# Converting 64-bit float weights inside an attention and MLP-mixer kernel: sign kept in the mantissa word, exponent masked in place, and the steps spread over four turns

## The chip, the cores and the metric

The kernel runs on one core of one Trainium2 chip. The metric is the device time of one execution in microseconds (us), as the median of several runs. Five engines of the core work side by side, each through its own list of instructions in order: TensorE (PE in the profile; PEld is its weight load), VectorE (DVE), ScalarE (ACT), GpSimd (POOL) and SyncE (SP). In this kernel SP issues nearly all the DMAs. An engine that meets an instruction whose input isn't ready stands still with everything behind it in its list.

## The reference

```python
def _attn_ref(q, k, v, g_q, g_k):                 # batch 8, heads 12, seq 448, head_dim 64
    q_n, k_n = rmsnorm(q, g_q), rmsnorm(k, g_k)
    scores = 1.0 / np.sqrt(64) * q_n @ k_n.transpose(0, 1, 3, 2)
    attn = softmax(scores)
    return attn @ v
def _moe_ref(x, w_tok1, w_tok2, w_ch1, w_ch2):    # x: the heads side by side, 8 x 448 x 768
    h = np.maximum(x.transpose(0, 2, 1) @ w_tok1, 0.0) @ w_tok2
    u = x + h.transpose(0, 2, 1)
    return u + np.maximum(u @ w_ch1, 0.0) @ w_ch2
```

(Shortened; the softmax has its maximum subtracted.) q, k and v are float32. The four weights are float64: `w_tok1` 448 x 256, `w_tok2` 256 x 448, `w_ch1` 768 x 1536 and `w_ch2` 1536 x 768. The kernel sees their bits as 64-bit integers, and has to make float32 of them itself.

## The kernel before

All 48 pairs of heads (six for each batch element) go through attention; each batch element then goes through the token layers (`tok1`, `tok2`) and the two channel layers. For batch element 0 the channel layers are plain products (`first_stage`, 36 of them); for the seven others they are a scheme with seven products of sums of blocks (`ch1`, `ch2`), for which sums of weight blocks must lie in DRAM. Attention for batch element b+1 runs in between the mixer work of element b. TensorE, VectorE, ScalarE and GpSimd get their instructions in the order in which the code emits them. Lists of work items are woven into each other by `merge`, by the costs written beside the items. SP's own queue is ordered by the scheduler of the framework.

**The weight conversion.** The weights come in 40 chunks of at most 128 rows and 512 numbers: chunks 0 to 3 are `w_tok1` and `w_tok2`, chunks 4 to 39 feed the 36 plain products of batch element 0 ("stage n" is chunk n+4). A chunk lies in one of five `raw` buffers as pairs of 32-bit words, so that the low words and the high words each lie 8 bytes apart. Per chunk there are six computing steps:

1. VectorE, line 263, *mask*: mantissa bits of the high word, with the implied one, into `cv_sb` (two buffers).
2. VectorE, line 264, *sum*: low word times 2^-32 plus that mantissa, into the low word.
3. VectorE, line 266, *exponent*: exponent bits of the high word into the same `cv_sb` buffer, which lies packed.
4. ScalarE, line 274, *shift of the exponent*: a Relu with scale 8 and a bias, in place in `cv_sb`.
5. VectorE, line 281, *sign*: sign bit of the high word joined to the result of step 4, into the high word.
6. VectorE, line 308, *product*: low word times 2^-20 times high word, into the float32 stage.

`weight_items` makes "turns" of these. Turn i issues, in this order: the load of chunk i+2 (line 176, on SP, two DMAs; the buffer is that of chunk i-3), sign of chunk i-2, mask, sum and exponent of chunk i, shift of chunk i-1, product of chunk i-2, and the store of the stage of chunk i-3 to DRAM (line 192, on SP).

Turns 0 to 13 are woven into the first attention steps. In `first_items`, five turns (14 to 18) are woven into the token layers of batch element 0; the others are hung on the 36 products: turn 19+k behind product number `begins(k)`, from k = 0 to 23. Stage k+13 is so made at place k, well ahead of its product at first and a few products ahead at the end. The last six products are woven with the last sums of weight blocks (`sum_items`): GpSimd forms them (lines 204 to 207), SP sends them out (line 211) and fetches earlier stages back (line 240).

Other lines that the steps below touch: 391 the exponentials on ScalarE, 361 and 739 transposes on TensorE, 387, 440 and 460 its attention products, 761 and 769 its token products, 774 the addition of a token product on VectorE, 857 the plain products on TensorE, 866 and 867 the copy (ScalarE) and the addition (GpSimd) of their results, 1314 and 1322 to 1325 the start of an inverse root on VectorE and its three Newton steps on GpSimd, 349 the scaling that uses it, 428 the sums of exponentials, 978 the transposes of a finished output on VectorE, 722 the fetch of x for the token layers.

Of the kernel before, what the change touches and what calls it, by code (L numbers as in the profile page):

```python
# [8 lines left out]
F32 = mybir.dt.float32  # L9
U32 = mybir.dt.uint32  # L10
I32 = mybir.dt.int32
I64 = mybir.dt.int64
AF = mybir.ActivationFunctionType
ALU = mybir.AluOpType
# [12 lines left out]
def merge(*lists):  # L27

    totals = [sum(c for c, _ in l) or 1.0 for l in lists]
    done = [0.0] * len(lists)  # L30
    at = [0] * len(lists)
    res = []
    while True:
        live = [i for i in range(len(lists)) if at[i] < len(lists[i])]
        if not live:
            return res
        i = min(live, key=lambda i: (done[i] + lists[i][at[i]][0] / 2) / totals[i])
        c, fn = lists[i][at[i]]
        at[i] += 1
        done[i] += c  # L40
        res.append((c, fn))
# [3 lines left out]
def whole(ctx, tc, shifted, pre, q, k, v, g_q, g_k, moe_w_tok1, moe_w_tok2, moe_w_ch1, moe_w_ch2, out):  # L45


    nc = tc.nc
# [51 lines left out]
    ident, one_c, expo_c, g_t = pre.ident, pre.one_c, pre.expo_c, pre.g_t  # L100
# [3 lines left out]
    cv_sb = const.tile([P, 2, WCOLS], F32, name="cv_sb")  # L104
# [5 lines left out]
    st = dict(pre.st)  # L110
# [43 lines left out]
    def columns(i):  # L154
        src = chunks[i][1][0]
        return WCOLS if chunks[i][2] is None or len(src.shape) == 3 else src.shape[-1]
# [4 lines left out]
    def weight_load(i):  # L161
        rows, srcs, dst = chunks[i]
        wide = srcs[0].dtype == I64
        t = raw_tile()
        flat = t[0:rows].rearrange("p n w -> p (n w)")
        if not wide:
            t = t[:].rearrange("p n w -> p (n w)").bitcast(F32)
            flat = t[0:rows]
        n = columns(i) // len(srcs) * (1 + wide)
        for k, src in enumerate(srcs):  # L170
            to = flat[:, k * n:(k + 1) * n]
            if wide:
                src = src.bitcast(U32)
            if len(src.shape) == 3:
                to = to.rearrange("p (i n) -> p i n", i=src.shape[1])
            nc.sync.dma_start(out=to, in_=src)
        st["raw", i] = t

    def slots(j, lo, hi):

        w, group, m, t = stages[j]
        if group < 3:
            a = ws1[group, lo:hi, :, t, m % 2, :]
        elif group == 3:
            a = ws3[lo:hi, :, t, :]
        else:
            a = ws2[t // 3, lo:hi, :, t % 3, m, :]
        return a.rearrange("q p n -> p q n")

    def store(j):  # L190

        nc.sync.dma_start(out=slots(j, 0, 4), in_=st["stage", j])
# [4 lines left out]
    def sum_items():  # L197
# [39 lines left out]
        def one(i):  # L237
            if i < len(order):
                t = st["sum", order[i]] = raw_tile()
                nc.sync.dma_start(out=eight(t)[:, 0:4], in_=slots(order[i], 0, 4))  # L240
            if 0 <= i - 2 < len(order):
                q = eight(st["sum", order[i - 2]])
                make(q, q)
            if 0 <= i - 3 < len(order):
                send(order[i - 3])
                load_units(st["at"])

        def eight(t):
            if len(t.shape) == 4:
# [3 lines left out]
                [(1.0, lambda i=i: direct(i)) for i in range(n - 6, n + 1)],  # L253
                [(1.0, lambda i=i: one(i)) for i in range(len(order) + 3)])

    def convert_first(i):

        if chunks[i][1][0].dtype != I64:
            return
        rows, n = chunks[i][0], columns(i)  # L260
        lo, hi = (st["raw", i][0:rows, 0:n, w] for w in range(2))
        e = cv_sb[0:rows, i % 2, 0:n].bitcast(U32)
        nc.vector.tensor_scalar(e, hi, 0x000FFFFF, 0x00100000, ALU.bitwise_and, ALU.bitwise_or)  # L263
        nc.vector.scalar_tensor_tensor(  # L264
            out=lo.bitcast(F32), in0=lo, scalar=2.0**-32, in1=e, op0=ALU.mult, op1=ALU.add)
        nc.vector.tensor_scalar(e, hi, 0x7FF00000, None, ALU.bitwise_and)
        st["cv", i] = e

    def convert_second(i):

        if chunks[i][1][0].dtype != I64:
            return
        rows, n, e = chunks[i][0], columns(i), st["cv", i]
        nc.scalar.activation(out=e, in_=e, func=AF.Relu, bias=expo_c[0:rows, 0:1], scale=8.0)

    def convert_bits(i):

        if not 0 <= i < len(chunks) or chunks[i][1][0].dtype != I64:
            return
        hi, e = st["raw", i][0:chunks[i][0], 0:columns(i), 1], st.pop(("cv", i))  # L280
        nc.vector.scalar_tensor_tensor(  # L281
            out=hi, in0=hi, scalar=0x80000000, in1=e, op0=ALU.bitwise_and, op1=ALU.bitwise_or)

    def stage_home(j):


        if j == 8:
            st["stages"] = tu_pool.tile([P, 4, KC, HS], F32, name="stages", tag="tu")
        if 8 <= j < 13:
            o = (j - 8) * 4 * P  # L290
            return st["stages"][:].rearrange("p a b n -> p (a b n)")[:, o:o + 4 * P]
        if 13 <= j < 15:
            return h1_pool.tile([P, C], F32, name="stage", tag="h1")[:, 0:4 * P]
        t = unit_pool.tile([P, 3, 2, P], F32, name="stage", tag="unit")
        return t[:].rearrange("p t i n -> p (t i n)")[:, 0:4 * P]

    def convert_last(i):
        rows, srcs, dst = chunks[i]
        n = columns(i)
        if dst is None:  # L300
            dst = stage_home(i - len(first))
            st["stage", i - len(first)] = dst.rearrange("p (q n) -> p q n", q=4)
        t = st.pop(("raw", i))
        if srcs[0].dtype != I64:
            nc.gpsimd.tensor_copy(out=dst, in_=t[0:rows, 0:n])
        else:
            lo, hi = (t[0:rows, 0:n, w].bitcast(F32) for w in range(2))
            nc.vector.scalar_tensor_tensor(  # L308
                out=dst, in0=lo, scalar=2.0**-20, in1=hi, op0=ALU.mult, op1=ALU.mult)

    def weight_items(lo, hi):

        def one(i):
            if 3 <= i and i + 2 < len(chunks):
                weight_load(i + 2)
            convert_bits(i - 2)
            if i < len(chunks):
                convert_first(i)
            if 0 <= i - 1 < len(chunks):
                convert_second(i - 1)  # L320
            if 0 <= i - 2 < len(chunks):
                convert_last(i - 2)
            if 0 <= i - 3 - len(first):
                store(i - 3 - len(first))
        return [(1.0, lambda i=i: one(i)) for i in range(lo, hi)]


# [652 lines left out]
    def turns(b, cs, send=True):  # L980

        def one(cc):
            trans_y(b, cc)
            if send:
                later(2.0, lambda: send_y(b, cc, st.pop(("y", cc))))
        return [(0.3, lambda cc=cc: one(cc)) for cc in cs]

    def y_order(b):

        return [o * KC + m for m in ((0, 1, 2) if b else (2, 0, 1)) for o in range(2)]  # L990
# [31 lines left out]
    def first_items(tok, prods, some):  # L1022


        convert = weight_items(BEFORE, len(chunks) + 3)
        items = merge(tok, convert[:5])
        for j, it in enumerate(prods[:-6]):
            items.append(it)
            items += [(0.0, convert[5 + k][1]) for k in range(len(convert) - 5) if begins(k) == j]
            if j % 2 and j < 2 * len(some):  # L1030
                items.append(some[j // 2])
            if j in (26, 28):

                items += turns(0, [y_order(0)[j // 2 - 13]])
        return items, prods[-6:]

    def begins(k):


        return 2 + -(-k * 14 // 10) if k < 10 else min(k + 9, 29)  # L1040
# [14 lines left out]
    first, second = weight_chunks()  # L1055
    chunks = first + second
    AHEAD = 1
    BEFORE = len(first) + 10
# [12 lines left out]
    for p in (4, 5):  # L1071
# [7 lines left out]
        out=g_t[:, 0:1], in0=g_t[:, 0:1], scalar=float(D) ** 0.5, in1=g_t[:, 1:2],  # L1079
        op0=ALU.mult, op1=ALU.mult)  # L1080
# [26 lines left out]
    for b in range(B):  # L1107
# [20 lines left out]
        lo = (b + AHEAD) * per + 1  # L1128
# [12 lines left out]
        elif b + AHEAD < B:  # L1141
            t = (b + AHEAD) * NPAIR // 2
# [201 lines left out]
def kernel(  # L1344
# [30 lines left out]
    with tc.If(nc.values_load(small[0:1, 0:1], min_val=0, max_val=1,  # L1375
                              skip_runtime_bounds_check_because="a comparison's result") > 0) as arm:
        whole(tc, False, pre, *args)
    with arm.Else():
        whole(tc, True, pre, *args)
# [30 lines left out]
```

## Time and profile before

| | |
|---|---|
| median of 3 runs | 1311.29 us (1311.14 to 1311.92) |
| the profiled execution's own time | 1311.52 us |
| its span, first to last instruction | 1309.7 us |
| TensorE busy | 1263.6 us (96%) |
| VectorE busy | 764.4 us (58%) |
| ScalarE busy | 372.1 us (28%) |
| GpSimd busy | 352.8 us (27%) |
| first and last mask of the conversion | 24.7 and 257.0 us |

Some 1.8 us of the profiled time lie outside its span. The conversion lives in the first 263 us; the remaining 1047 us are seven rounds of mixer and attention that do not touch it. A row of a timeline is: start (us from the span's start), duration (us), engine, line, operation, output and inputs, shapes, count; in brackets the idle time of the engine before it and what ended it. [...]

### The profile page before, as it was taken

What the parts mean: (1) busy time and instruction counts of PE and PEld (TensorE: products, weight loads), DVE (VectorE), ACT (ScalarE), POOL (GpSimd) and SP (SyncE); (2) the same over time, 40 slices, a digit from 0 to 9 for tenths busy, and PEclk for the clock granted to TensorE, in tenths of its full rate; (3) what the DMA queues carried; (4) which work ended last, traced back from release to release, by engine and by line L of the source; (5) the groups of instructions that cost most, each with busy time, mean ns of one, the idle gap of its engine ahead of it and who ended that gap; (6) DMA issues with size and microseconds to landing.
All of it is one profiled execution on the core that took longest, in us unless ns stands there. A gap on an engine that the chain in (4) does not pass through costs nothing.

```text
span 1309.7 us, 20218 instructions
## 1 busy us (share of the span) xinstructions
PE 1263.6 (96%) x7408; PEld 930.4 (71%) x7408; DVE 764.4 (58%) x1205; ACT 372.1 (28%) x740; POOL 352.8 (27%) x575
## 2 busy tenths in 40 slices
PE   5999999799998999999999999999999999999997
PEld 3344444347687688796778777896788868797996
DVE  6888688937684466645665366654756266433212
ACT  5562433213331134302441044302332033200100
POOL 1203230357342122221332122321232123111220
PEclk9999999899999999999999999999999999999998
DMA  9664487999989676695648667684767865386554
GB/s 212 170 185 134 135 212 177 202 258 252 245 195 233 149 184 160 147 232 118 160 128 222 152 147 178 162 226 101 169 156 166 212 139 141 116 217 135 174 172 91
DMA packets 502449, 228.06 MB, mean 174 GB/s; under 512 B 374532, under 2 KB 464004, under 8 KB 502340
## 3 DMA queue, kind: packets, MB, share of 16 engines
q1 hardware_dynamic: 489218, 224.83, 69.7%
q10 hardware_dynamic: 12994, 1.84, 0.8%
q8 instruction: 61, 1.00, 0.3%
q14 instruction: 48, 0.39, 0.1%
q0 software_dynamic: 128, 0.00, 0.0%
HBM read 187.07 MB, written 39.52 MB: 173 GB/s over the span
## 4 chain that ended last, share of the span: by engine, by line
PE 79%; DVE 8%; DMA 5%; SPq 3%; issue 2%; ACT 1%; POOL 1%; DVEq 0%; ACTq 0%; POOLq 0%
PE m_ps L885 25%; PE m_ps L942 24%; PE o_ps L460 8%; PE s_ps L387 8%; PE m_ps L769 5%; PE m_ps L761 5%; DVE raw L264 1%; PE m_ps L857 1%; PE d_ps L440 1%; DVE raw L281 1%; DMA raw<-in_moe_w_ch_dram 1%; DMA qk_t<-in_k_dram 1%; PE m_ps L440 1%; DVE cv_sb L263 1%; DVE stage L308 1%
## 5 line engine op out<-in xcount | busy, mean ns | idle before, releaser
L942 PE MATMUL m_ps<-hb,unit 128*128 128x224 f32 x1764 | 339.8, 353 | 3.6 <-DMA unit<-ws 1.9
L942 PEld LDWEIGHTS m_ps<-hb,unit 128*128 128x128 f32 x1764 | 332.2, 190 | 14.7 <-issue 12.7
L885 PE MATMUL m_ps<-tu,unit 128*128 128x224 f32 x1008 | 202.0, 355 | 0.1
L885 PEld LDWEIGHTS m_ps<-tu,unit 128*128 128x128 f32 x1008 | 188.9, 190 | 14.8 <-issue 9.2
L391 ACT ACTIVATE e<-s_ps 128x448 f32<-128x448 f32 x294 | 138.1, 549 | 199.7 <-PE s_ps L387 191.5
L885 PE MATMUL m_ps<-uT,unit 128*128 128x224 f32 x756 | 151.2, 354 | 1.0 <-DVE hb L890 1.0
L885 PEld LDWEIGHTS m_ps<-uT,unit 128*128 128x128 f32 x756 | 142.2, 190 | 8.1 <-issue 4.6
L387 PE MATMUL s_ps<-qkT 64*64 64x448 f32 x1260 | 142.0, 545 | 0.0
L460 PE MATMUL o_ps<-e,v 64*64 64x448 f32 x1148 | 131.1, 538 | 0.1
L428 DVE TENSOR_TENSOR es<-es,e 128x896 f32<-128x896 f32 x90 | 109.0, 1212 | 16.6 <-ACT e L391 11.9
L951 POOL TENSOR_TENSOR uT<-uT,r 128x448 f32<-128x448 f32 (+1 forms) x56 | 56.6, 1020 | 228.8 <-DVE r L951 142.7
L890 DVE TENSOR_TENSOR r<-m_ps,r 128x448 f32<-128x448 f32 x63 | 39.2, 622 | 108.3 <-PE m_ps L885 56.2
L951 DVE TENSOR_TENSOR uT<-uT,m_ps 128x448 f32<-128x448 f32 (+1 forms) x70 | 33.7, 499 | 111.2 <-PE m_ps L942 111.2
L387 PEld LDWEIGHTS s_ps<-qkT 64*64 64x64 f32 x1260 | 44.8, 132 | 66.5 <-issue 58.5
L460 PEld LDWEIGHTS o_ps<-e,v 64*64 64x64 f32 x1148 | 45.8, 133 | 63.9 <-issue 59.0
L890 POOL TENSOR_TENSOR hb<-r,r 128x448 f32<-128x448 f32 x21 | 24.6, 1173 | 234.1 <-ACT r L906 234.1
L761 PE MATMUL m_ps<-x,w_sb 112*128 112x384 f32 x256 | 84.5, 487 | 1.0 <-ACT x L741 1.0
L769 PE MATMUL m_ps<-w_sb,h 128*128 128x448 f32 x192 | 75.2, 544 | 3.3 <-DVE uT L774 3.3
L761 PEld LDWEIGHTS m_ps<-x,w_sb 112*128 112x128 f32 x256 | 48.4, 190 | 34.3 <-ACT x L741 1.3
L891 ACT ACTIVATE hb<-hb 128x448 f32<-128x448 f32 x63 | 36.3, 577 | 116.4 <-DVE hb L890 97.2
L1292 DVE TENSOR_REDUCE ms<-sq 128x28 f32<-128x896 f32 (+2 forms) x44 | 47.5, 1079 | 34.1 <-ACT sq L1278 31.3
L857 PE MATMUL m_ps<-hb,stage 128*128 128x448 f32 x144 | 57.2, 556 | 8.0 <-ACT r L866 8.0
(122 smaller groups left out, 1352.7 us busy)
## 6 DMA issues: line engine op xcount, KB each, us to landing
unit<-ws SPq DMA_DIRECT2D x294, 384.0 KB, 4.1
raw<-in_moe_w_ch_dram SPq DMA_DIRECT2D x72, 256.0 KB, 3.6
v<-in_v_dram SPq DMA_DIRECT2D x96, 112.0 KB, 3.7
xs<-xt SPq DMA_DIRECT2D x56, 168.0 KB, 4.6
x<-xs SPq DMA_DIRECT2D x14, 672.0 KB, 7.3
out_dram<-turned SPq DMA_DIRECT2D x168, 56.0 KB, 2.0
qk_t<-in_q_dram SPq DMA_DIRECT2D x144, 56.0 KB, 3.5
qk_t<-in_k_dram SPq DMA_DIRECT2D x144, 56.0 KB, 3.8
```

Of the source, the lines that this page charges most:

```text
L387: nc.tensor.matmul(out=pss[i][rows_of(i, a), 0:S], lhsT=qkT[h, 1, k * D:(k + 1) * D], rhs=qkT[h, 0, :], start=True, stop=True)
L391: nc.scalar.activation(out=e[:, i, :], in_=pss[i][:, 0:S], func=AF.Exp)
L428: nc.vector.tensor_tensor(out=es[:], in0=(es if k > 1 else st["e", t, 0])[:], in1=st["e", t, k][:], op=ALU.add)
L460: nc.tensor.matmul(out=st["o", p][a * D:(a + 1) * D, 0:S], lhsT=vt[rows, k * D:(k + 1) * D], rhs=e[rows, :], **kw)
L761: nc.tensor.matmul(out=ps[:, 0:HC], lhsT=w1_sb[0:R, c, jc * P:(jc + 1) * P], rhs=st["x", b, h][0:R, :, c, :], start=(c == 0), stop=(c == N ...
L769: nc.tensor.matmul(out=ps[:, 0:S], lhsT=st["h1", jc][:, cc * P:(cc + 1) * P], rhs=w2_sb[:, jc].rearrange("p c r -> p (c r)"), start=(jc == ...
L857: nc.tensor.matmul(out=ps, lhsT=a[:, o + 2 * half, :], rhs=natural(half)[:, :, t, :] if wide else u[:, half * KC + t, :], start=(t == 0 an ...
L885: nc.tensor.matmul(out=ps[:, j * HS:(j + 1) * HS], lhsT=w[:, t, j, :], rhs=m, start=(t == 0), stop=(t == KC - 1))
L890: add = lambda e, o, x, y: e.tensor_tensor(out=o, in0=x, in1=y, op=ALU.add)
L942: nc.tensor.matmul(out=ps[:, j * HS:(j + 1) * HS], lhsT=st["w"](j, t), rhs=hb[:, HB[what], t, :], start=(t == 0), stop=(t == KF - 1))
L951: add = lambda e, o, x, y: e.tensor_tensor(out=o, in0=x, in1=y, op=ALU.add)
L1292: self.nc.vector.tensor_reduce(out=st["ms", p][:, p % 2, lo:hi], in_=sq[:, lo:hi], axis=AX_X, op=ALU.add)
```

## The change

The sign goes into the low word right after the sum, and the exponent is masked in place in the high word; the `cv_sb` buffer then serves only between mask and sum. The shift on ScalarE works in place in the high word, two turns behind the mask (it was one). The product stands at the head of the turn, three turns behind the mask (it was two, at the turn's end), ahead of the load into the buffer that it frees. The store follows one turn later, so that there is one turn more; six turns (14 to 19) are woven into the token layers instead of five, and turn 20+k stands at place k.

```diff
     def convert_first(i):
-        rows, n = chunks[i][0], columns(i)
-        lo, hi = (st["raw", i][0:rows, 0:n, w] for w in range(2))
-        e = cv_sb[0:rows, i % 2, 0:n].bitcast(U32)
-        nc.vector.tensor_scalar(e, hi, 0x000FFFFF, 0x00100000, ALU.bitwise_and, ALU.bitwise_or)
-        nc.vector.scalar_tensor_tensor(
-            out=lo.bitcast(F32), in0=lo, scalar=2.0**-32, in1=e, op0=ALU.mult, op1=ALU.add)
-        nc.vector.tensor_scalar(e, hi, 0x7FF00000, None, ALU.bitwise_and)
-        st["cv", i] = e
+        if wide(i):
+            lo, hi = words(i)
+            m = cv_sb[0:chunks[i][0], i % 2, 0:columns(i)].bitcast(U32)
+            nc.vector.tensor_scalar(m, hi, 0x000FFFFF, 0x00100000, ALU.bitwise_and, ALU.bitwise_or)
+            nc.vector.scalar_tensor_tensor(
+                out=lo.bitcast(F32), in0=lo, scalar=2.0**-32, in1=m, op0=ALU.mult, op1=ALU.add)
+            nc.vector.scalar_tensor_tensor(
+                out=lo, in0=hi, scalar=0x80000000, in1=lo, op0=ALU.bitwise_and, op1=ALU.bitwise_or)
+            nc.vector.tensor_scalar(hi, hi, 0x7FF00000, None, ALU.bitwise_and)
 
     def convert_second(i):
-        nc.scalar.activation(out=e, in_=e, func=AF.Relu, bias=expo_c[0:rows, 0:1], scale=8.0)
-
-    def convert_bits(i):
-        nc.vector.scalar_tensor_tensor(
-            out=hi, in0=hi, scalar=0x80000000, in1=e, op0=ALU.bitwise_and, op1=ALU.bitwise_or)
+        if wide(i):
+            e = words(i)[1]
+            nc.scalar.activation(out=e, in_=e, func=AF.Relu, bias=expo_c[0:chunks[i][0], 0:1], scale=8.0)
...
     def weight_items(lo, hi):
         def one(i):
+            if 0 <= i - 3 < len(chunks):
+                convert_last(i - 3)
             if 3 <= i and i + 2 < len(chunks):
                 weight_load(i + 2)
-            convert_bits(i - 2)
-            if i < len(chunks):
-                convert_first(i)
-            if 0 <= i - 1 < len(chunks):
-                convert_second(i - 1)
-            if 0 <= i - 2 < len(chunks):
-                convert_last(i - 2)
-            if 0 <= i - 3 - len(first):
-                store(i - 3 - len(first))
+            convert_first(i)
+            convert_second(i - 2)
+            if 0 <= i - 4 - len(first):
+                store(i - 4 - len(first))
...
-        convert = weight_items(BEFORE, len(chunks) + 3)
-        items = merge(tok, convert[:5])
+        convert = weight_items(BEFORE, len(chunks) + 4)
+        items = merge(tok, convert[:6])
         for j, it in enumerate(prods[:-6]):
             items.append(it)
-            items += [(0.0, convert[5 + k][1]) for k in range(len(convert) - 5) if begins(k) == j]
+            items += [(0.0, convert[6 + k][1]) for k in range(len(convert) - 6) if begins(k) == j]
```

`words(i)` gives the low and the high words of chunk i, `wide(i)` says whether chunk i exists and is 64-bit.

More of the change, by code (lines that the diff above doesn't have):

```diff
@@ L254, in sum_items, with wide, words @@
                 [(1.0, lambda i=i: one(i)) for i in range(len(order) + 3)])
+    def wide(i):
+        return 0 <= i < len(chunks) and chunks[i][1][0].dtype == I64
+    def words(i):
+        return [st["raw", i][0:chunks[i][0], 0:columns(i), w] for w in range(2)]
     def convert_first(i):
-        if chunks[i][1][0].dtype != I64:
-            return
-        rows, n = chunks[i][0], columns(i)
-        lo, hi = (st["raw", i][0:rows, 0:n, w] for w in range(2))
-        e = cv_sb[0:rows, i % 2, 0:n].bitcast(U32)
-        nc.vector.tensor_scalar(e, hi, 0x000FFFFF, 0x00100000, ALU.bitwise_and, ALU.bitwise_or)
-        nc.vector.scalar_tensor_tensor(
-            out=lo.bitcast(F32), in0=lo, scalar=2.0**-32, in1=e, op0=ALU.mult, op1=ALU.add)
-        nc.vector.tensor_scalar(e, hi, 0x7FF00000, None, ALU.bitwise_and)
-        st["cv", i] = e
-    def convert_second(i):
[L271 to L274, printed above, removed]
-    def convert_bits(i):
[L278 to L281, printed above, removed]
-            out=hi, in0=hi, scalar=0x80000000, in1=e, op0=ALU.bitwise_and, op1=ALU.bitwise_or)
+        if wide(i):
[7 more added lines that the diff above has]
+            nc.vector.tensor_scalar(hi, hi, 0x7FF00000, None, ALU.bitwise_and)
+    def convert_second(i):
+        if wide(i):
+            e = words(i)[1]
+            nc.scalar.activation(out=e, in_=e, func=AF.Relu, bias=expo_c[0:chunks[i][0], 0:1], scale=8.0)
     def stage_home(j):
@@ L302, in convert_last @@
             st["stage", i - len(first)] = dst.rearrange("p (q n) -> p q n", q=4)
[L303 to L307, printed above, removed]
+        if wide(i):
+            lo, hi = (w.bitcast(F32) for w in words(i))
             nc.vector.scalar_tensor_tensor(
                 out=dst, in0=lo, scalar=2.0**-20, in1=hi, op0=ALU.mult, op1=ALU.mult)
+        else:
+            nc.gpsimd.tensor_copy(out=dst, in_=st["raw", i][0:rows, 0:n])
+        st.pop(("raw", i))
     def weight_items(lo, hi):
         def one(i):
+            if 0 <= i - 3 < len(chunks):
+                convert_last(i - 3)
             if 3 <= i and i + 2 < len(chunks):
                 weight_load(i + 2)
-            convert_bits(i - 2)
-            if i < len(chunks):
-                convert_first(i)
-            if 0 <= i - 1 < len(chunks):
-                convert_second(i - 1)
-            if 0 <= i - 2 < len(chunks):
-                convert_last(i - 2)
-            if 0 <= i - 3 - len(first):
-                store(i - 3 - len(first))
+            convert_first(i)
+            convert_second(i - 2)
+            if 0 <= i - 4 - len(first):
+                store(i - 4 - len(first))
         return [(1.0, lambda i=i: one(i)) for i in range(lo, hi)]
```

## The prediction

> **What bounds the kernel now.** I read the page first, then busy time by stretch, then TensorE's own timeline for the places where it stands still. Columns of the stretches: length, then PE, PEld, DVE, ACT and POOL busy (instructions), PE clock, DMA share, GB/s.
>
> ```profile
> 20.00:85.00 65.00, 59.67 (x563) 28.58 (x558) 54.61 (x94) 39.79 (x80) 10.20 (x32) 1.00 0.73 191
> 85.00:123.30 38.30, 36.15 (x205) 17.60 (x204) 34.09 (x50) 17.60 (x35) 9.82 (x20) 1.00 0.46 131
> 123.30:199.00 75.70, 75.63 (x340) 34.83 (x336) 54.37 (x80) 27.91 (x52) 19.88 (x36) 1.00 0.69 183
> 199.00:263.00 64.00, 55.96 (x192) 26.38 (x189) 58.49 (x99) 16.84 (x32) 14.06 (x16) 0.95 0.80 188
> ```
>
> TensorE is full from 123 to 199 us and nearly full elsewhere; VectorE comes close in 85 to 123 (89%) and 199 to 263 (91%). So time can be won only where TensorE idles, and VectorE must not be pushed where it is full. TensorE's idle places that have to do with the conversion:
>
> ```profile
> 53.35 1.90 PE L361 MATMUL t_ps<-ident,hb 112*128 112x112 f32 x16 [2.31 <-ACT e L391]
> ...
> 231.74 12.29 PE L857 MATMUL m_ps<-hb,stage 128*128 128x448 f32 x32
> 250.66 20.05 PE L857 MATMUL m_ps<-hb,stage 128*128 128x448 f32 x48 [6.63 <-ACT r L866]
> ```
>
> Both idles are ended by ScalarE. Its timeline says why ScalarE was late:
>
> ```profile
> 52.15 0.72 ACT L274 ACTIVATE cv_sb<-cv_sb,expo_c 128x512 uint32<-128x512 uint32 x1 [2.56 <-DVE cv_sb L266]
> ...
> 249.47 0.72 ACT L274 ACTIVATE cv_sb<-cv_sb,expo_c 128x512 uint32<-128x512 uint32 x1 [8.22 <-DVE cv_sb L266]
> 250.10 0.94 ACT L866 COPY r<-m_ps 128x448 f32<-128x448 f32 x2
> ```
>
> ScalarE stands 8.22 us before a shift whose exponent VectorE has not made; the copies that free TensorE's result buffers are queued behind. In all, the table of waits from 20 to 270 us has this pair at 41.7 us in 14 waits. Most of it costs nothing; at TensorE I count 1.1 us at 27 (same cause, ScalarE waits 3.19), 2.3 at 51, 0.6 at 73, and the 6.63 at 244. The last has a sequel:
>
> ```profile
> 231.74:234.84 3.10, 3.10 (x8) 1.62 (x9) 1.00 1.08 256
> 250.66:253.76 3.10, 3.10 (x4) 1.51 (x5) 0.50 0.92 158
> ```
>
> Behind the gap the clock is 0.50, and 4 matmuls of line 857 begin in 3.10 us instead of 8: about 1.6 us more.
>
> **VectorE's work per turn.** One turn where nothing else intervenes:
>
> ```profile
> 230.24 0.70 DVE L281 SCALAR_TENSOR_TENSOR raw<-raw,cv_sb 128x512 uint32<-128x512 uint32 x1
> 230.98 0.43 DVE L263 TENSOR_SCALAR cv_sb<-raw 128x512 uint32<-128x512 uint32 x1
> 231.45 0.69 DVE L264 SCALAR_TENSOR_TENSOR raw<-raw,cv_sb 128x512 f32<-128x512 uint32 x1
> 232.18 0.43 DVE L266 TENSOR_SCALAR cv_sb<-raw 128x512 uint32<-128x512 uint32 x1
> 232.52 0.68 DVE L308 SCALAR_TENSOR_TENSOR stage<-raw 128x512 f32<-128x512 f32 x1
> 233.12 0.69 DVE L281 SCALAR_TENSOR_TENSOR raw<-raw,cv_sb 128x512 uint32<-128x512 uint32 x1
> ```
>
> From start to start: sign 0.74, mask 0.47, sum 0.73, exponent 0.34, product 0.60: 2.88 us. An instruction that needs the one just before it starts 0.04 us after its end; one that doesn't starts some 0.09 before. The new order is product 0.60, mask 0.47, sum 0.73, sign 0.74 (it reads the sum), exponent 0.34 if the next instruction is free of it: again 2.88. Five operations are removed and five added per chunk; the sum is zero.
>
> Unknown is the exponent mask written in place, 8 bytes apart. No row has it. Nearest is line 263, which reads words 8 bytes apart at 0.43; writing so costs the other form nothing (0.69 for line 264, 0.68 for the packed output of 308). [...] I take 0.43. ScalarE's shift in place 8 bytes apart: 0.72 now; up to twice that would still be hidden, with ScalarE at 28% and its result needed a turn later.
>
> **20 to 85 us.** ScalarE's shift is two turns old: its waits vanish, for 1.1 + 2.3 + 0.6 = 4.0 us at TensorE. VectorE can follow, since it waits for TensorE 1.71 us at 61 and 3.02 at 82. The two first turns lack the old sign and product, but carry the new sign: 0.8 us more by turn 2, inside that slack. Bounds: gain 0 to 4.7; I take 4.0.
>
> **85 to 123 us, the sixth turn.** 2.88 us of VectorE work come into a full stretch. Its place matters as well:
>
> ```profile
> 108.20 2.29 DVE L349 TENSOR_TENSOR qk_t<-qk_t,rs 112x1024 f32<-112x1024 f32 x1 [2.72 <-POOL rs L1325]
> ```
>
> Between line 1314 and this scaling GpSimd takes 5.5 us for its Newton steps, and a turn (102.5 to 105.4) now lies in that wait. In the built order the weaving puts it ahead of line 1314, so that the wait is bare: another 2.9. VectorE is 5.7 later here against its own start. TensorE feels it through line 774: token products 3 and 6 wait for additions. Followed through, the 4.0 of before make the plain products start at 123.3, where they start now: gain and loss cancel. Without the 4.0 they would start at 127.4.
>
> **123 to 243 us.** Full; nothing gained. Loads: each is issued behind the product that frees its buffer, which moved from the end of one turn to the start of the next. Issue 1.2 us and landing 3.6 make 4.8, and the mask comes two turns (5.8) later: hidden by a microsecond; uncovered, it is a wait like the 3.03 us before the mask at 189.49. q and k loads queued behind it on SP would slip with it; in the built order those of 81 us have moved ahead of it. Stores keep their places. All 72 and 36 of them remain.
>
> **243 to 293 us.** The shift at 249.47 needs an exponent made by 241, so the copies follow the product at once: 0.5 us instead of 6.6, and no half clock: 6.1 + 1.6 = 7.7 us. VectorE must keep pace: its waits for loads (2.25 us from 233 to 239) should go with the load one place earlier, and the last three turns are a product alone. Stages 31 to 35 come at 245.6, 248.4, 252.9, 253.5, 254.2; TensorE wants them from 247 every 3.1 us. Token products then start at 262.8 instead of 270.6. What is late next is the chain behind:
>
> ```profile
> 270.53 0.45 POOL L204 TENSOR_TENSOR raw<-stage 128x128 f32<-128x128 f32 x1 [3.83 <-DMA ws<-raw]
> ...
> 278.24 0.45 POOL L204 TENSOR_TENSOR raw<-raw 128x128 f32<-128x128 f32 x1 [5.89 <-DMA raw<-ws]
> ...
> 281.77 2.22 POOL L867 TENSOR_TENSOR uT<-uT,r 128x448 f32<-128x448 f32 x2
> ```
>
> Only after line 867 do the transposes (978) and additions (774) run, and TensorE's token product at 285.23. That chain hangs on SP: line 722 at 263.34 behind the last xs piece, which follows a transpose at 254.7 behind turn k=19. That turn ends 4.2 us sooner, so TensorE goes on at 281.0. It has then idled from 276.2, 4.8 us. By the row above, the clock falls after such a gap (0.75 over the 6.5 us of it: halfway); the 2.31 us at 51 left it at 1.00. [...] Without the fall the gain is 4.2, with it 2.6. The new gap is nearer 6.6 than 2.3: I take 2.6. From 293 on TensorE is full and passes it on.
>
> **Sum.** -4.0 + 4.0 - 7.7 + 3.5 (chain) + 1.6 (clock) = -2.6: 1311.5 - 2.6 = 1308.9 for the profiled run, 1308.7 against the median.
>
> **Rivals.**
> - *The chain gives nothing back*, its DMAs being late anyway (share 0.92 from 263 to 293): 1311. For it: landing times there are 4 to 6.6 us. 0.14.
> - *The whole tail arrives*, 7.7 us, if SP is free sooner than I think: 1303.7. Against it: the transfers of the chain are serial. 0.14.
> - *The sixth turn decides, slower*: with VectorE full from 85 to 123, 4.1 us come in unless the first stretch pays for them. Over 1.5 us of missing payment is slower than before; with none, -2.6 + 4.1: 1312.8. For it: VectorE is 84% busy before 85 and may hold TensorE there. 0.18.
> [...]
>
> My forecast has 0.44; its own range is 1307 to 1310.5. Range for all: 1304.5 to 1313.8. No change is within 0.2%, 2.6 us, about what a measurement of this kernel can tell. The forecast lies on that bound: 0.24 faster, 0.20 same; with the rivals faster 0.42, same 0.28, slower 0.30.
>
> **What would show it.** No ScalarE wait for the exponent; no gap at 244 and clock 1.00 there; exponent at 0.43; a wait of 5.6 us before the scaling at line 349; plain products starting at 123; token product 3 of element 1 near 281 behind a gap of 4 to 5 us. Wrong if masks wait for loads in earnest, or TensorE starts its plain products after 125.

## The result, and the profile after

| | before | changed |
|---|---|---|
| median, runs taken side by side | 1311.39 us (1310.35 to 1315.56, 13 runs) | 1309.48 us (1306.44 to 1311.39, 13 runs) |
| ratio | | 0.9976, 95% interval 0.9965 to 0.9987 |
| own time of the profiled execution | 1311.52 us | 1311.39 us |
| its span | 1309.7 us | 1309.6 us |

By the ratio the change makes the kernel faster by 0.24% (3.1 us, the distance of the two means); the medians are 1.9 us apart, 0.15%. One thing must be kept in mind below: the profiled execution of the changed kernel is the slowest of its 13, and its span is only 0.1 us shorter than that of before. Its trace shows which waits went and which came, but hardly the gain of the median; the two accounts are kept apart.

The stretches of before, in the changed kernel (that from 123 to 199 us, full in both, is left out). The columns are the stretch and its length, then busy time of TensorE, its weight loads, VectorE, ScalarE and GpSimd (instructions in brackets), the granted clock, the DMA share and GB/s:

```profile
20.00:85.00 65.00, 63.42 (x594) 30.21 (x590) 58.89 (x102) 42.65 (x82) 12.76 (x32) 1.00 0.74 188
85.00:123.30 38.30, 33.67 (x184) 16.56 (x177) 32.48 (x48) 16.76 (x33) 7.35 (x20) 0.96 0.62 174
...
199.00:263.00 64.00, 59.73 (x201) 28.13 (x200) 55.08 (x94) 17.70 (x32) 16.64 (x24) 0.97 0.73 172
263.00:293.00 30.00, 25.25 (x80) 13.02 (x82) 6.98 (x14) 3.37 (x7) 13.93 (x28) 0.94 0.93 265
```

TensorE is busy 3.75 us longer in the first stretch and 3.77 in the one from 199 us. It is busy 2.48 less in the second, and 3.56 less in the last, where it had 28.81 before. (Busy time is not work alone: behind the wait near 220 us, at a clock of 0.81 over the whole of them, 16 products are busy for 7.74 us that took 6.28 before, at 1.00.) Three stretches show a clock below 1.00 where before it was one (0.95 from 199 to 263 us).

ScalarE's timeline of the changed kernel (start, duration, engine, line, operation; in brackets what it waited for):

```profile
52.61 0.79 ACT L279 ACTIVATE raw<-raw,expo_c 128x512 uint32<-128x512 uint32 x1
...
244.35 0.53 ACT L860 COPY r<-m_ps 128x448 f32<-128x448 f32 x1 [2.64 <-PE m_ps L851]
245.85 0.53 ACT L860 COPY r<-m_ps 128x448 f32<-128x448 f32 x1 [0.97 <-PE m_ps L851]
```

The shift (line 279, 274 before) no longer waits near 52 us, and the copies of 244 us (line 860, 866 before) wait for TensorE's product alone. Over the run the 128x512 shifts stand 13.6 us before an unmade exponent, where it was 38.5. What is left (5.16, 3.22, 2.50 and 2.74 us, from 230 to 254 us) lies where turns follow one another and ScalarE has no other work; no wait of TensorE ends there.

TensorE's timeline of the changed kernel:

```profile
112.73 3.16 PE L763 MATMUL m_ps<-w_sb,h 128*128 128x448 f32 x4 [2.62 <-DVE uT L768]
...
222.63 7.74 PE L851 MATMUL m_ps<-hb,stage 128*128 128x448 f32 x16 [2.77 <-ACT r L860]
...
239.59 15.41 PE L851 MATMUL m_ps<-hb,stage 128*128 128x448 f32 x40
256.50 9.29 PE L851 MATMUL m_ps<-hb,stage 128*128 128x448 f32 x24 [1.50 <-DVE stage L302]
...
283.87 7.84 PE L763 MATMUL m_ps<-w_sb,h 128*128 128x448 f32 x16 [4.75 <-DVE uT L768]
```

The gap at 244 us, 6.63 before, is gone: the row of 239.59 runs through it. But four other waits stand here that were shorter or absent. The stretches behind three of them, and the one behind the vanished gap, by clock:

```profile
112.60:115.70 3.10, 2.97 (x5) 1.21 (x6) 3.07 (x6) 0.00 (x0) 0.73 (x2) 0.56 0.49 93
222.60:225.70 3.10, 3.07 (x5) 1.51 (x6) 3.07 (x3) 1.83 (x3) 2.79 (x2) 0.52 1.01 192
...
245.60:248.70 3.10, 3.10 (x10) 1.61 (x9) 3.07 (x6) 1.38 (x2) 2.10 (x3) 1.00 0.82 188
...
283.80:286.90 3.10, 3.03 (x4) 1.51 (x5) 1.38 (x4) 0.00 (x0) 2.94 (x8) 0.50 1.09 383
```

In these two executions one half clock (0.50 behind the gap of before) has been exchanged for three (0.56, 0.52 and 0.50). The price is in the timeline: the 16 products at 222.63 took 7.74 us where 16 took 6.28 before, and the 16 at 283.87 took 7.84 where it was 6.28.

Put together, this is where TensorE stands against before, by the start of the same work in the two traces. Plain products are counted by the trace's records, 288 of them, eight for each of the 36, of which the code has four matmuls each:

| work that starts | before, us | changed, us | difference |
|---|---|---|---|
| transposes ahead of the first token products | 83.07 | 79.05 | -4.02 |
| first plain product | 123.28 | 123.57 | +0.29 |
| plain product 24 | 136.55 | 135.20 | -1.35 |
| plain product 120 of 288 | 184.38 | 182.93 | -1.45 |
| plain product 192, behind the wait near 220 | 222.36 | 222.63 | +0.27 |
| plain product 208 | 231.74 | 233.47 | +1.73 |
| plain product 248, behind the old gap | 255.51 | 248.61 | -6.90 |
| first token product of element 1 | 270.55 | 265.62 | -4.93 |
| token product 3 of element 1 | 285.23 | 283.87 | -1.36 |
| attention behind the token products | 291.44 | 291.64 | +0.20 |
| fast products behind the wait near 420 | 421.14 | 420.24 | -0.90 |

At each of these rows up to product 248 TensorE has the same numbers of matmuls of each kind behind it in both kernels. From 421 us on no wait of TensorE is left in either trace, and the difference stays at 0.90.

### The profile page after: what moved, and what is told of

Its sections match the earlier page's. It is cut to its first block, busy times and chain, and to the rows that moved or that the text cites. A ratio compares the mean times of both kernels' runs of the same rounds, so it can differ in the third digit from the quotient of the medians.

```text
span 1309.6 us, 20269 instructions
## 1 busy us (share of the span) xinstructions
PE 1264.2 (97%) x7408; PEld 930.7 (71%) x7408; DVE 763.4 (58%) x1205; ACT 373.5 (29%) x740; POOL 350.6 (27%) x575
## 4 chain that ended last, share of the span: by engine, by line
PE 79%; DVE 9%; DMA 4%; SPq 3%; issue 2%; ACT 1%; POOL 1%; DVEq 0%; ACTq 0%; POOLq 0%
PE m_ps L936 25%; PE m_ps L879 25%; PE s_ps L381 8%; PE o_ps L454 8%; PE m_ps L763 5%; PE m_ps L755 5%; PE m_ps L851 3%; DVE raw L269 1%; DVE raw L271 1%; PE d_ps L434 1%; DMA qk_t<-in_k_dram 1%; DMA raw<-in_moe_w_ch_dram 1%; DVE stage L302 1%; DVE ms L1286 1%; DMA hb<-in_q_dram 1%
## 5 line engine op out<-in xcount | busy, mean ns | idle before, releaser
L763 PE MATMUL m_ps<-w_sb,h 128*128 128x448 f32 x192 | 78.3, 561 | 8.9 <-DVE uT L768 8.9
L763 PEld LDWEIGHTS m_ps<-w_sb,h 128*128 128x128 f32 x192 | 36.5, 195 | 46.8 <-issue 27.8
```

What stands on the lines that cost most here:

```text
L763: nc.tensor.matmul(out=ps[:, 0:S], lhsT=st["h1", jc][:, cc * P:(cc + 1) * P], rhs=w2_sb[:, jc].rearrange("p c r -> p (c r)"), start=(jc == ...
```

## Experiments

Each ran beside the kernel before, in a series in which that one took 1314.8 us (median of 25 runs, 1312.27 to 1318.78), and not 1311.39. The ratios are therefore compared, not the times; the changed kernel itself was not run again in this series.

### ScalarE one turn behind again

```diff
-            convert_second(i - 2)
+            convert_second(i - 1)
```

> The changed kernel with ScalarE's shift one turn behind the mask again instead of two; the new operations, the product three turns behind and the sixth turn stay. Theory (the age of the shift is what took TensorE's waits away): the stalls of 1.5 and 2.8 us near 27 and 50 us and the gap of 5 to 7 us near 244 us are back, with the clock at half behind the latter; token product 3 of element 1 comes at 285 or later; 1312 to 1315 us. Rival (the age of the product, or the sign's new place, did it): no gap at 244, within 1 us of the changed kernel's 1309.5.

Measured: 1322.32 us (5 runs), ratio 1.0057 (1.0043 to 1.0070), that is, 0.8% above the changed kernel's 0.9976. The direction is the theory's, the size twice what it said. ScalarE's timeline of this kernel:

```profile
53.56 0.76 ACT L279 ACTIVATE raw<-raw,expo_c 128x512 uint32<-128x512 uint32 x1 [2.54 <-DVE raw L273]
...
257.66 0.77 ACT L279 ACTIVATE raw<-raw,expo_c 128x512 uint32<-128x512 uint32 x1 [8.17 <-DVE raw L273]
258.32 0.94 ACT L860 COPY r<-m_ps 128x448 f32<-128x448 f32 x2
```

And TensorE's:

```profile
54.79 3.07 PE L355 MATMUL t_ps<-ident,hb 112*128 112x112 f32 x16 [2.75 <-ACT e L385]
...
258.89 20.44 PE L851 MATMUL m_ps<-hb,stage 128*128 128x448 f32 x48 [5.49 <-ACT r L860]
```

Both waits of the kernel before are back, in the same words: a shift of 8.17 us's waiting, two copies behind it, TensorE behind these. So it is the age of the shift that takes them away, and the rival, that the product's age or the sign's place does it, falls. On why the loss is larger than forecast the trace shows this much: the wait of 2.31 us at 51 of before is 2.75 here, and behind it the 16 transposes take 3.07 us instead of 1.90, at a clock of 0.73 from 53.60 to 56.70 us, where the kernel before had 1.00 from 53.30 to 56.40. The whole lag is there by the first token products (88.30, where the changed kernel has 80.72 and the kernel before 84.74), and the first plain product starts at 130.80 instead of 123.57. A likely reason for the longer waits, argued and not tried, is that the new order puts the exponent last in the turn, behind the sign. How the new operations would do on the old schedule, with five turns, was not tried either.

### Five turns in the token layers

```diff
-        items = merge(tok, convert[:6])
+        items = merge(tok, convert[:5])
...
-            items += [(0.0, convert[6 + k][1]) for k in range(len(convert) - 6) if begins(k) == j]
+            items += [(0.0, convert[5 + k][1]) for k in range(len(convert) - 5) if begins(k) == j]
```

> The changed kernel with five turns woven into the token layers instead of six; each later turn comes one place later among the plain products. Theory (the sixth turn and the bare Newton wait cost about 4 us between 85 and 123 us): the stalls of 2.1 and 2.8 us at 106 and 110 us shrink to under 1 us, no half clock follows, plain products start at 118 to 119 instead of 122; what of that is left at the end is set by the tail, 1306 to 1308.5 us. Rival (the turns are only put off, and the stage matrices come a turn later where TensorE already waits for them, at 219 and 254 us): plain products start as early, but TensorE stalls 2 to 3 us more there; 1309 to 1313 us.

Measured: 1313.14 us (12 runs), ratio 0.9986 (0.9975 to 0.9997), not told apart from the changed kernel's 0.9976 (0.9965 to 0.9987). TensorE's timeline of this kernel:

```profile
118.53 5.90 PE L851 MATMUL m_ps<-uT,stage 128*128 128x448 f32 x15
...
219.73 8.34 PE L851 MATMUL m_ps<-hb,stage 128*128 128x448 f32 x16 [5.17 <-ACT r L860]
...
244.76 3.25 PE L851 MATMUL m_ps<-hb,stage 128*128 128x448 f32 x8 [1.30 <-DVE stage L302]
```

The first half of the theory holds: the waits at 106 and 110 us are 1.25 and 0.98, no half clock follows, and plain products start 5.04 us sooner. Of these 0.80 was there already at the token products of 80 us (79.92 instead of 80.72), so the sixth turn costs TensorE 4.2 us in that stretch. The second half is the rival's: the turn is only put off. At 219.73 TensorE waits 5.17 us instead of 2.77, and three more waits for a stage matrix come (of 1.30, 0.46 and 0.24 us). Token products of element 1 start at 265.88, where they did with six turns (265.62). In this kernel the turn costs TensorE about the same on either side of the plain products.

### The last two residual additions on VectorE, in both kernels

The lines differ by six between the two kernels; the edit is the same:

```diff
-                to, c = u[:, o * KC + m, :], r_tile(1 + o)[:]
+                to = u[:, o * KC + m, :]
+                if n == len(stages) - 1:
+                    nc.vector.tensor_tensor(out=to, in0=to, in1=ps, op=ALU.add)
+                    continue
+                c = r_tile(1 + o)[:]
                 nc.scalar.copy(out=c, in_=ps)
                 nc.gpsimd.tensor_tensor(out=to, in0=to, in1=c, op=ALU.add)
```

In the changed kernel:

> The changed kernel with the two residual additions of the last pair of plain products taken from the PSUM tile by VectorE, instead of a ScalarE copy and a GpSimd addition behind the fetched sums. Theory (the chain over GpSimd gives the tail's gain back): the gap of 4.9 us at 279 us and the half clock behind it vanish; TensorE is 5 to 6.5 us earlier at 290 us, unless the unit matrices, issued at 282.5 us, are then what is late; 1304 to 1307.5 us. Rival (the DMAs of the sums and of the unit matrices set the pace anyway): the gap only moves to the first fast product, 1309 to 1310 us.

In the kernel before:

> The kernel before with the same two residual additions on VectorE. Theory: TensorE waits only 1.4 us for the chain there, so at most that is gained: 1310 to 1311.4 us; with the run above, the change is then worth 4 to 6 us where the chain over GpSimd is cut, instead of 1.9. Rival (the chain is no limit in either): both gain nothing, and the difference stays near 1.9 us.

Measured: 1311.72 us (7 runs) for the changed kernel, ratio 0.9965 (0.9951 to 0.9980); 1315.28 us (12 runs) for the kernel before, ratio 1.0006 (0.9993 to 1.0020). The first lies below the changed kernel's 0.9976, but the intervals overlap: that it beats it is not settled. The second is no gain, as both of its theories have it. Between the two the medians differ by 3.6 us and the ratios by 0.0041, some 5 us; the theory said 4 to 6. The rival said that the difference stays what it was, which is 1.9 us by the medians and 0.0024 by the ratios. With these intervals neither is excluded.

The traces say more than the times. TensorE's timeline with the additions on VectorE, changed kernel:

```profile
286.19 2.51 PE L883 MATMUL m_ps<-uT,unit 128*128 128x224 f32 x12 [0.47 <-DMA unit<-ws]
...
301.46 0.65 PE L883 MATMUL m_ps<-tu,unit 128*128 128x224 f32 x2 [1.12 <-POOL tu L786]
304.45 6.92 PE L883 MATMUL m_ps<-tu,unit 128*128 128x224 f32 x20 [2.35 <-POOL tu L786]
...
313.58 1.74 PE L454 MATMUL o_ps<-e,v 64*64 64x448 f32 x16
...
414.28 4.81 PE L940 MATMUL m_ps<-hb,unit 128*128 128x224 f32 x24 [3.17 <-DVE uT L949]
```

And kernel before with the same edit:

```profile
292.62 2.54 PE L889 MATMUL m_ps<-uT,unit 128*128 128x224 f32 x12
...
307.77 4.05 PE L889 MATMUL m_ps<-tu,unit 128*128 128x224 f32 x20 [0.58 <-POOL tu L792]
...
314.02 1.73 PE L460 MATMUL o_ps<-e,v 64*64 64x448 f32 x16
```

The gap at 279 is gone, and the fast products (line 883, 879 in the changed kernel) begin 6.43 us ahead of the same edit in the kernel before. At 313.58 against 314.02 this lead is 0.44. In the kernels without the edit the same attention starts at 314.60 (changed) and 314.56 (before): four kernels that come to the fast products between 286 and 294 us leave this stretch within 1.02 us of one another. Two things take the lead. The rows of 301.46 and 304.45 name the first: the moving sums of line 786 on GpSimd. The second is the clock behind these waits:

```profile
304.40:307.50 3.10, 3.04 (x8) 2.79 (x9) 0.00 (x0) 0.00 (x0) 3.02 (x8) 0.50 0.97 262
```

The 20 products of 304.45 take 6.92 us, those of 307.77 take 4.05. So the lead goes from 6.43 to 3.32 at the waits for the sums (304.45 against 307.77), and from 3.32 to 0.44 at the half clock behind them. GpSimd's timeline of the changed kernel with the edit:

```profile
297.88 0.70 POOL L204 TENSOR_TENSOR raw<-raw 128x128 f32<-128x128 f32 x1 [10.81 <-DMA raw<-ws]
...
303.75 0.65 POOL L786 TENSOR_TENSOR tu<-uT 128x224 f32<-128x224 f32 x1
```

And SP's queue there (start and time of its issues):

```profile
284.44 10.16 SPq L699 DMA_DIRECT2D out_dram<-turned  x8
294.65 0.48 SPq L240 DMA_DIRECT2D raw<-ws  x1
```

GpSimd stands 10.81 us before a fetched sum; SP issued it, the only fetch of a sum between 280 and 295 us, at 294.65, behind eight output pieces that took it from 284.44; and the moving sums that TensorE needs are queued behind on GpSimd. In the changed kernel the same fetch is issued at 295.28, in the kernel before at 296.27. So the chain of sums does take back a good part of what the tail gains, but not only by line 861 (867 before): remove that link and TensorE meets the same chain 20 us later. The 0.44 is not the end either: at 328 us the kernel before with the edit takes 3.48 us for eight attention products that take 0.93 in the changed one, since sums of exponentials and a load of v come late there, and its trace ends 2.7 us longer. The times of these two kernels therefore don't measure the chain alone. Whether the chain would give way if the output pieces left SP's queue, or whether the transfers themselves (the DMA share from 263 to 293 us is 0.93 in the changed kernel) would hold it, was not tried.

## Why the prediction was right, and where its steps were off

The time, 1308.7 against a measured 1309.48, and the sign are right, and so is the main mechanism: the older shift removes the wait of 244 us, and the chain of sums takes part of that back. Several steps between are off, and that their sum is right is in part luck. The steps, against the table above:

- **The turn on VectorE costs the same.** Right. In the changed kernel, where nothing intervenes:

```profile
227.44 0.68 DVE L302 SCALAR_TENSOR_TENSOR stage<-raw 128x512 f32<-128x512 f32 x1
228.04 0.42 DVE L268 TENSOR_SCALAR cv_sb<-raw 128x512 uint32<-128x512 uint32 x1
228.50 0.69 DVE L269 SCALAR_TENSOR_TENSOR raw<-raw,cv_sb 128x512 f32<-128x512 uint32 x1
229.22 0.69 DVE L271 SCALAR_TENSOR_TENSOR raw<-raw 128x512 uint32<-128x512 uint32 x1
229.95 0.43 DVE L273 TENSOR_SCALAR raw<-raw 128x512 uint32<-128x512 uint32 x1
230.30 0.69 DVE L302 SCALAR_TENSOR_TENSOR stage<-raw 128x512 f32<-128x512 f32 x1
```

  From product to product 2.86 us; predicted was 2.88. The exponent written in place, 8 bytes apart, takes 0.43, as the packed one did (0.476 against 0.469 in the mean of all 128x512 chunks). The chances also held 0.10 for one that takes the 0.69 of the sum and the sign all along, which was the author's estimate; no run shows it. ScalarE's shift in place takes 0.786 in the mean instead of 0.732; VectorE's products wait for it twice, 1.9 us in all, between 123 and 199 us, where TensorE is busy for 75.37 of 75.70.
- **20 to 85 us, -4.0.** Measured -4.02.
- **85 to 123 us, +4.0.** Measured +4.31 (from -4.02 to +0.29), and 4.2 by the experiment with five turns: the right size. The plain products start at 123.57; predicted was 123.3. The path there is another. The wait before the scaling is

```profile
105.07 2.30 DVE L343 TENSOR_TENSOR qk_t<-qk_t,rs 112x1024 f32<-112x1024 f32 x1 [3.89 <-POOL rs L1319]
```

  3.89 us, not 5.6. The wait is bare, as foreseen, but the 5.5 us were read off a stretch in which VectorE worked a turn beside GpSimd's Newton steps; without it they take 3.9. The profile of before had that figure too: its next such scaling, at 155.06, stands bare and waits 3.89. In place of the missing 1.7 us a turn (108.96 to 112.15) now lies between the scaling and the addition of line 768, and holds token product 6 back: TensorE's 2.62 us at 110, which costs a half clock besides (4 products in 3.16 us instead of 1.77).
- **123 to 243 us, nothing.** The first step that failed: TensorE gains 1.74 here and loses 3.18. The gain is at the first attention work behind the plain products, the kernel before first and then the changed one:

```profile
134.05 2.57 PE L460 MATMUL o_ps<-e,v 64*64 64x448 f32 x8
...
131.23 0.93 PE L454 MATMUL o_ps<-e,v 64*64 64x448 f32 x8
```

  Before, the loads of v that these products need are issued from 131.08 on and land some 3.9 us later, so that the eight products drag; in the changed kernel they are issued from 124.58 on and have landed. The prediction called this stretch full and had not seen these 1.64 us. Why SP comes to the loads sooner is not pinned, so this gain is luck. The loss comes near 220 us. ScalarE's timeline of the changed kernel:

```profile
196.69 0.95 ACT L1272 ACTIVATE sq<-qk_t 128x896 f32<-128x896 f32 x1 [6.97 <-DMA raw<-in_moe_w_ch_dram]
...
220.85 0.67 ACT L361 ACTIVATE qkT<-qkT,g_t 128x448 f32<-128x448 f32 x1 [2.43 <-DVE qkT L358]
222.07 0.94 ACT L860 COPY r<-m_ps 128x448 f32<-128x448 f32 x2
```

  TensorE waits for the two copies. They are queued behind a scaling (line 361) that waits for VectorE's transposes, and those stand behind a turn. All of this is the same in the kernel before, in the same order, with the copies at 221.80: TensorE comes 1.09 us sooner (the products ahead start at 213.58 instead of 214.67) to a chain that is 0.27 later, so the wait of 1.41 becomes 2.77. The half clock behind it costs 1.46, and 0.33 went before, where TensorE waits at 198.22 behind the square of 196.69. VectorE can't start that chain sooner: it stands 4.14 us before exponentials that ScalarE runs behind the same square. The loads, too, were not hidden. From 123 to 199 us the masks wait 9.06 us for them, where it was 3.18, a sign that the prediction had named for being wrong; it does not show at TensorE, since VectorE has those 4.14 us to spare.
- **243 to 293 us, -7.7.** The gap and its half clock gave 8.6 (from +1.73 to -6.90). Stage 33 then came too late: predicted for 252.9, its product began at 255.77, and TensorE, that waited 1.50, is back to -4.93. Two terms make the 2.9 us. The waits for loads, 2.25 us from 233 to 239 before, were to go and are still 1.73, so that the product at 246.89 is already 1.3 late. And the turns before stage 33 had been put at 2.88 us each, but GpSimd's additions and sums run beside them. VectorE's timeline of the changed kernel:

```profile
246.89 1.26 DVE L302 SCALAR_TENSOR_TENSOR stage<-raw 128x512 f32<-128x512 f32 x1
...
249.38 0.83 DVE L271 SCALAR_TENSOR_TENSOR raw<-raw 128x512 uint32<-128x512 uint32 x1
250.25 0.56 DVE L273 TENSOR_SCALAR raw<-raw 128x512 uint32<-128x512 uint32 x1
250.73 0.94 DVE L302 SCALAR_TENSOR_TENSOR stage<-raw 128x512 f32<-128x512 f32 x1
```

  From product to product 3.84 us: the product at 246.89 lies beside GpSimd's addition of 246.46 to 247.60, the rest beside its sums of 248.23 to 251.12. Beside them the sum and the sign take 0.83 instead of 0.69, the exponent 0.56 instead of 0.43, and the products 1.26 and 0.94 instead of 0.68 and 0.69; what makes them longer is not shown. With 3.84 and 3.52 for the last two whole turns the sum of this step would have been 1.6 smaller. The profile of before showed this as well: beside GpSimd's additions its sum of 251.13 took 1.51 and its exponent of 252.68 took 1.24, and the last two turns ahead of the transpose of 254.70 took 7.57 us together (from 247.13), no less than in the changed kernel (7.36).
- **The chain gives 3.5 back, and 1.6 go to the clock.** Measured 3.57 (from -4.93 to -1.36) and 1.56. The right size, at another place: tail and chain are both some 2.9 us later than predicted. GpSimd's timeline of the changed kernel:

```profile
276.88 0.46 POOL L204 TENSOR_TENSOR raw<-raw 128x128 f32<-128x128 f32 x1 [5.07 <-DMA raw<-ws]
...
280.42 2.21 POOL L861 TENSOR_TENSOR uT<-uT,r 128x448 f32<-128x448 f32 x2
```

  Line 861 comes 1.35 us sooner than before, where 4.2 were predicted. The transpose behind the last turn, on which SP's queue waits, came at 254.25 instead of 254.70, since VectorE was late by the previous point; the rest of the way, in the changed kernel mostly transfers (10.1 us) and SP's issues (9.0), took 26.2 us instead of 27.1.
- **From 293 us on TensorE is full and passes it on.** Wrong. The prediction did not count two waits that the profile of before has:

```profile
414.46 4.81 PE L942 MATMUL m_ps<-hb,unit 128*128 128x224 f32 x24 [1.64 <-DVE uT L951]
421.14 4.02 PE L942 MATMUL m_ps<-hb,unit 128*128 128x224 f32 x20 [1.88 <-DMA unit<-ws]
```

  In the changed kernel there is nothing to pass on at 293 us, where TensorE is 0.20 late. It is 1.46 ahead at 349 us, where before waits 0.99 and it doesn't, and falls back to 0.74 at 414, where it waits 2.37. The experiment with the additions on VectorE shows that a real lead isn't passed on whole: of 6.43 us there, 3.1 went to the moving sums and 2.9 to the half clock. By the same reading a lead of 7.7 us, the rival in which the whole tail arrives, would have met the same sums; how much of it would have come through is not shown.

In the sum of the trace, then, the terms are -4.02, +4.31, -1.74, +3.18, -8.63, +1.97, +3.57, +1.56 and, behind 293 us, -1.10: -0.90 at TensorE's last product, for a predicted -2.6. (The span keeps only 0.1 of it; the last output writes end later.) The median does better than this one execution. Executions of either kernel lie up to 5 us apart (4.95 and 5.21), and why stays open, since one of each has a trace; falls of the clock that come in one execution and not in another would do it, but that is not shown. That the forecast time came out right owes something to terms that were wrong in both directions.

## What to carry to other kernels

Here a consumer in a strict queue that worked on data one turn old stood idle where the producer was put behind other work (ScalarE for 8.22 us, and behind it TensorE for 6.63); one more turn of age removed every such wait of TensorE, without a change in work. Before a gain is passed on to the end, look for the next place where the gaining engine would meet a chain of another pace, even one that shows no wait now, or a short one: near 220 us TensorE came 1.09 us sooner to a chain that did not, and the wait grew by that and the chain's own 0.27, from 1.41 to 2.77 us. And a duration read beside another engine's work was not the duration without it, in either direction: the Newton steps got faster alone (3.9 us instead of 5.5), the turns slower in company (3.84 us instead of 2.86).

## What the runs showed of the hardware beyond that

The half clock did not go by the length of one idle here. Stretches right behind an idle of TensorE (columns as above): two of the changed kernel with the additions on VectorE, behind 2.02 and 3.17 us; then the kernel before with the same additions, behind 2.42 us at the place where the kernel before idled 2.31:

```profile
221.20:224.30 3.10, 3.10 (x5) 1.54 (x6) 3.07 (x3) 1.71 (x3) 2.72 (x2) 0.56 0.96 180
...
414.20:417.30 3.10, 3.02 (x16) 3.02 (x17) 2.14 (x5) 0.34 (x1) 2.45 (x9) 1.00 0.16 27
...
53.25:56.48 3.23, 3.23 (x20) 2.95 (x23) 3.13 (x6) 2.83 (x6) 0.00 (x0) 0.51 0.72 226
```

An idle of 2.02 us left the clock at 0.56, one of 3.17 left it at 1.00. At 51 us the 2.31 us of before left it at 1.00, and the prediction went by that; with 2.42 us at the same place it was 0.51 (0.97 from 20 to 85 us, where before had 1.00), and the 16 transposes took 3.23 us instead of 1.90. Near 414 us idles of 2.78 us (the kernel before with the additions on VectorE) and 3.28 us (five turns) were followed by 0.73 and 0.53 over 3.1 us, while the 3.17 us was not. So the length alone did not decide: idles of 2.02, 2.42 and 2.78 us were followed by a fall, and one of 3.17 was not. What decides is not shown, and a sum can't count on an idle of 2 to 3 us being free of a fall. In the changed kernel each fall cost 1.4 to 1.6 us, on top of waits of 2.6 to 4.8; at 304 us, with the additions on VectorE, one cost 2.9.
